# Projecting the first unit, and half of the last, with the weights stationary

## Chip, cores and metric

The kernel runs on one core of a Trainium2 chip. The metric is the device time of one execution in microseconds (us). Engines are named as in the profile: PE is TensorE, the matrix engine (PEld its weight loads), ACT is ScalarE, DVE is VectorE, POOL is GpSimd and SP is SyncE, which here issues transfers only.

## The reference

A causal convolution over 7 tokens, one softmaxed set of weights for each of 8 heads (24 channels each), and then a gated feed-forward layer. Input x is 8 x 4096 x 192 in float32, the output 32768 x 192.

```
w = softmax(weight)                               # 8 heads x 7 taps
x_pad = 6 rows of zeros ahead of each sequence of x
c[b,s,h,g] = sum_k w[h,k] * x_pad[b, s+k, h*24+g]
c = c.reshape(32768, 192)
out = (maximum(c @ w_gate, 0) * (c @ w_val)) @ w_out     # 192 -> 1536 -> 192
```

## The kernel before

Tokens go in 16 units (u = 0 to 15). A unit is 1024 tokens of one sequence and the same 1024 tokens of the sequence four batches on; the two are the "streams" st = 0, 1, kept in the upper and lower 64 partitions. A unit has two windows w of 512 tokens. The 1536 inner columns are NFF = 12 blocks f of 128.

*Gates* (gate_val, line 550). For each window and each f, six matmuls a stream (three 64-row chunks c for Wg, three for Wv) fill two tiles of PSUM. ACT takes the relu (line 561, tile gr), DVE multiplies it by the second tile (line 562) into hT, the inner activations, transposed. In units 1 to 14 the matmuls are cut into 64x64 tiles of the array (M = 64), in units 0 and 15 into 64x128 tiles (M = 128).

*Projection.* In units 1 to 14 (project_across) Wo is the stationary operand and hT moves, 512 tokens at a time, in 64x64 tiles: piece 0 gives the first 128 output columns of window 0, piece 1 those of window 1, piece 2 the last 64 columns of both. A piece has two turns (cross_pass, line 658): in each, the two halves of the rows write to different banks, and the second turn swaps the banks. Between the turns stands an empty instruction on SP that waits for the first turn's last matmul and lets the second start. The result comes out transposed, so it is copied as 16-bit words (line 680, "words"), written to a DRAM tile "held" (keep), read back by a transposing transfer (turn_back, line 698) and stored (send, line 708). Piece 1 is first copied raw by ACT and DVE (lines 736 and 737) and sorted into words by POOL during the next unit's gates. The transposing transfers and the stores are issued in the next unit, by SP in program order.

In units 0 and 15 (project) hT is stationary and Wo, 192 columns wide, moves (half_pass, line 579, 64x128 tiles); the result has tokens on partitions, is copied (evict, put, line 605) and stored (line 606) at once. The second window of unit 15 is done in whole 128x128 tiles (whole_half, line 628) at the very end, behind its first window's passes.

*Convolution.* For the next unit's tokens, ACT starts a sum (lane_first, line 508) and DVE continues it for the first 576 tokens of each unit (lane_rest, line 522); for the other 448, products of tap and shifted x are made by ACT, DVE (VECTOR, line 494) and, in unit 1, POOL (FOR_POOL), and POOL adds them (add, line 498) into xc. The shifted x comes from x_e, sorted by POOL into x_p (line 472) and transposed by SP's transfers into x_r (line 476). The last 448 tokens of unit 1 are instead convolved on PE during unit 0's projection, in two tiles "x" and "y" of two turns each (conv_turn_of, line 411), cast by ACT (conv_out, line 436) and transposed into xc by SP (conv_turn, line 460). The products' tile "prods" has one buffer, "x_h" (words and raws) two, PSUM four tiles "ps" of two banks.

The order on every engine is the order in which the code is written out; nothing is rescheduled. In unit 0 the projection runs: first window's stream 0 and the turns of the convolution mixed, then the other three, with ACT's products cut into portions (work).

Of the kernel before, what the change touches and what calls it, by code (L numbers as in the profile page):

```python
# [17 lines left out]
def kernel(  # L18
# [23 lines left out]
    WIN = 512  # L42
# [1 line left out]
    SUB = 112  # L44
    VECTOR = [(0, 5), (1, 5), (2, 5), (0, 6), (2, 1)]
    NOW = 2
    FOR_POOL = [(1, 6), (2, 6)]
    GSUB = 5
    DSUB = 104

# [349 lines left out]
    def conv_turn_of(g, t, wide, turn, after):  # L400


        xt = xts[g]
        n = len(GROUPS[g][1])
        W = 2 * n * G
        for slot in range(2):
            for r in range(2):
                bank = r ^ turn
                h = HEADS[t][bank][slot]
                rows = slice(64 * r, min(64 * r + 64, SUB + PAD))  # L410
                mm = nc.tensor.matmul(  # L411
                    out=wide[:, bank, W * slot : W * (slot + 1)],
                    lhsT=wide_bands[h][rows, :],
                    rhs=xt[rows, 0:n, :, G * h : G * (h + 1)],
                    start=(turn == 0 and slot == 0),
                    stop=(turn == 1),
                    tile_position=(64 * r, 0),
                    skip_group_check=True,
                )
                if after is not None:  # L420
                    tc.add_manual_dep(mm.ins, after.ins.name, SYNC, reason="same banks, other rows")
                    after = None
        if turn == 0:
            done = nc.sync.nop()
            tc.add_manual_dep(done.ins, mm.ins.name, SYNC, reason="first turn over")
            return done
# [105 lines left out]
            for c, k in VECTOR[:now]:  # L532
                product(nc.vector, v, c, k)

    def gate_val(u, w):
        h = hpool.tile([128, NFF, 2, WIN], F16, name="hT")
        xcb = xc[u]
        for f in range(NFF):
            if u == 0 and w == 0 and f == 5:
                second_block()  # L540
            pss = [psum.tile([128, 2, 512], FP, name="ps") for _ in range(2)]
            order = [(i, c) for i in range(2) for c in range(NCH)]
            if u == 0 and w == 0 and f == 0:
                order = [(i, c) for c in range(NCH) for i in range(2)]
            M = 64 if 0 < u < NUNIT - 1 else 128
            for i, c in order:
                W = (Wg, Wv)[i]
                for st in range(2):
                    for m in range(0, 128, M):
                        nc.tensor.matmul(  # L550
                            out=pss[i][m : m + M, st, :],
                            lhsT=W[64 * st : 64 * st + 64, c, 128 * f + m : 128 * f + m + M],
                            rhs=xcb[64 * st : 64 * st + 64, c, WIN * w : WIN * (w + 1)],
                            start=(c == 0),
                            stop=(c == NCH - 1),
                            tile_position=(64 * st, m),
                        )
            by_stream = u == 0 and w == 0 and f < 2
            for sts in (slice(0, 1), slice(1, 2)) if by_stream else (slice(0, 2),):
                gr = gpool.tile([128, 2, WIN], F16, name="gr")  # L560
                nc.scalar.activation(out=gr[:, sts], in_=pss[0][:, sts], func=ACTF.Relu)  # L561
                nc.vector.tensor_tensor(  # L562
                    out=h[:, f, sts], in0=gr[:, sts], in1=pss[1][:, sts], op=ALU.mult
                )
        return h
# [81 lines left out]
    def cross_pass(piece, hs, ps, turn, after):  # L647


        for f in range(NFF):  # L650
            for r in range(2):
                bank = r ^ turn
                for half in range(2):
                    if piece == 2:
                        w, st, d = bank, half, 128
                    else:
                        w, st, d = piece, bank, 64 * half
                    mm = nc.tensor.matmul(  # L658
                        out=ps[bank][64 * half : 64 * half + 64],
                        lhsT=Wo[64 * r : 64 * r + 64, f, d : d + 64],  # L660
                        rhs=hs[w][64 * r : 64 * r + 64, f, st, :],
                        start=(turn == 0 and f == 0),
                        stop=(turn == 1 and f == NFF - 1),
                        tile_position=(64 * r, 64 * half),
                        skip_group_check=True,
                    )
                    if after is not None:
                        tc.add_manual_dep(mm.ins, after.ins.name, SYNC, reason="same banks, other rows")
                        after = None
        return turn_over(turn, mm)  # L670
# [6 lines left out]
        return done  # L677

    def words(copy, pt, src):
        copy(out=pt[:], in_=src[:].bitcast(U16).rearrange("p b (t l) -> p b l t", l=2))  # L680

    def keep(u, i, pt):
        flat = pt[:].rearrange("p b l t -> p b (l t)")
        if i < 2:
            nc.sync.dma_start(
                out=planes[u][i, :, 0:128, :].rearrange("s c e -> c s e"), in_=flat
            )
            return
        for st in range(2):
            nc.sync.dma_start(  # L690
                out=planes[u][:, st, 128:D, :].rearrange("w c e -> c w e"),
                in_=flat[64 * st : 64 * st + 64],
            )

    def turn_back(u, i):
        w, st = i // 2, i % 2
# [7 lines left out]
    def send(u, i):  # L704
        w, st = i // 2, i % 2
        bp, w0 = u * UNIT // S, u * UNIT % S // WIN
        row0 = (bp + NB * st) * S + WIN * (w0 + w)
        nc.sync.dma_start(
            out=bass.AP(
                tensor=out.tensor,  # L710
                offset=out.offset + row0 * D,
                ap=[[D, 128], [128 * D, 4], [1, D]],
            ),
            in_=across.pop((u, i))[:],
        )

    def project_across(u, hs, work):
        planes[u] = dram.tile([2, 2, D, 2 * WIN], U16, name="held")
# [25 lines left out]
            for c, k in VECTOR[NOW:]:  # L744
                product(nc.vector, u + 1, c, k)

    def project(u, hs, work, y=None):
        bp, w0 = u * UNIT // S, u * UNIT % S // WIN
        at, done = {}, {}
        order = [(0, 0), (1, 0), (0, 1), (2, 0), (1, 1), (3, 0), (2, 1), (3, 1)]  # L750
        if u == 0:
            order = [(0, 0), ("x", 0), (1, 0), ("x", 1), ("y", 0), (0, 1), ("y", 1), (1, 1)]
            order += [(2, 0), ("out", 1), (3, 0), (2, 1), (3, 1)]
        if u == NUNIT - 1:
            order = [(0, 0), (1, 0), (0, 1), (1, 1), (2, 2), (3, 2)]
        rows0 = [(bp + NB * (i % 2)) * S + WIN * (w0 + i // 2) for i in range(4)]

        def fetch(i):
# [1 line left out]
                product(nc.scalar, u + 1, c, k)  # L760

        for i, turn in order:
            if i == "out":
                fetch(turn)
                evict(at[turn][0], rows0[turn], False)
                continue
            if i in ("x", "y"):
                t = int(i == "y")
                if turn == 0:
                    at[i] = psum.tile([128, 2, 512], FP, name="ps")  # L770
                elif t == 0:
                    fetch(0)
                done[i] = conv_turn_of(2, t, at[i], turn, done.get(i))
                if turn:
                    conv_out(2, t, at[i], y)
                continue
            h, st = hs[i // 2], i % 2
            row0 = rows0[i]
            if turn == 2:
# [1 line left out]
                continue  # L781
            if turn == 0:
                at[i] = slots()
            elif u > 0 or i > 1:
                fetch(i)
            done[i] = half_pass(h, st, at[i][1], turn, done.get(i))
            if turn and (u, i) != (0, 1):
                evict(at[i][0], row0, i == 3)


# [25 lines left out]
    for u in range(NUNIT):  # L816
# [8 lines left out]
        if 0 < u < NUNIT - 1:  # L825
            load_rest(lane_turn(u + 1))
        if u - 1 in planes:
            pt = ypool.tile([128, 2, 2, WIN], U16, name="y")
            words(nc.gpsimd.tensor_copy, pt, raws.pop(u - 1))
            keep(u - 1, 1, pt)  # L830
            turn_back(u - 1, 0)
            turn_back(u - 1, 1)
            send(u - 1, 0)
# [12 lines left out]
            for k in range(2, KW):  # L846
                add(u, k)
        while len(hs) < 2:
            hs.append(gate_val(u, len(hs)))
        del xc[u]  # L850
        work = [[] for _ in range(4)]
        if u + 1 < NUNIT:
            begun = lane_first(u + 1)
            if u == 0:
                flat = ypool.tile([128, ROOM], F16, name="y")
                y = flat[:, 0 : GSUB * NCH * 128].rearrange("p (j c s r) -> p j c s r", j=GSUB, c=NCH, s=2)
                load_rest(lane_load(2, begun))
            lane_rest(u + 1, len(VECTOR) if u in (0, NUNIT - 2) else NOW)
        if u + 2 < NUNIT:
            todo = [(c, k) for k in (0, 1, 2, 3, 4, 6) for c in range(NCH)]  # L860
            todo = [ck for ck in todo if ck not in VECTOR + (FOR_POOL if u == 0 else [])]
            cuts = [0, 5, 10, 15, 16] if u == 0 else [0, 10, 16, 16]
            work = [todo[a:b] for a, b in zip(cuts, cuts[1:])]
        if 0 < u < NUNIT - 1:
            project_across(u, hs, work)
        else:
            project(u, hs, work, y if u == 0 else None)
        if u == 0:
            conv_turn(2, y)

# [29 lines left out]
```

## Time and profile before

| | us |
|---|---|
| runs before | 762.23, 763.25, 769.23; median 763.25 |
| the profiled execution | 761.7 |
| its span on the core | 759.9 |
| PE busy | 756.1 (99%) |
| DVE busy | 707.4 (93%) |
| ACT busy | 617.3 (81%) |
| POOL busy | 404.9 (53%) |
| granted TensorE clock | 1.0 |

Busy times are those of the profiled execution. A PE that is busy all the time says that PE's work and its waits set the time; the other engines matter where PE waits for them. "A <- B" in a row names what ended an engine's idle time; the number behind x is a count of instructions.

### The profile page before, as it was taken

To read this page: it belongs to the slowest core of one execution; us is meant where nothing else is said; L and a number is where in the kernel's file an instruction comes from. 1 tells how busy PE (TensorE), PEld (TensorE's weight loads), DVE (VectorE), ACT (ScalarE), POOL (GpSimd) and SP (SyncE) were. 2 spreads that over 40 slices of the span, in tenths; PEclk is the share of its full clock that TensorE was granted. 3 is DMA by queue.
4 is the path that set the end of the run, shared out by engine and by line. 5 is a ranking of instruction groups with operands and counts; after the bars stand their busy time and mean duration, and the time that the engine had idled before them with its cause. 6 is when DMAs were issued, how large, how long until landed. Compare 5 with 4: busy or idle time off the path is not lost.

```text
span 759.9 us, 30608 instructions
## 1 busy us (share of the span) xinstructions
PE 756.1 (99%) x13623; PEld 484.0 (64%) x13623; DVE 707.4 (93%) x768; ACT 617.3 (81%) x719; POOL 404.9 (53%) x263
## 2 busy tenths in 40 slices
PE   9999999999999999999999999999999999999998
PEld 5495555555666666666666666666666776666548
DVE  7998999999999999999999999999999999999891
ACT  6887887978879798897988879788798887976671
POOL 9519449094580936819276291863908548091000
PEclk9999999999999999999999999999999999999999
DMA  9969029688395894949759498594957939654732
GB/s 118 132 113 136 16 68 157 162 107 181 94 184 146 91 180 105 190 128 105 195 93 184 119 138 180 81 186 114 170 145 100 189 98 160 140 107 113 185 87 85
DMA packets 231308, 100.33 MB, mean 132 GB/s; under 512 B 185288, under 2 KB 220424, under 8 KB 231176
## 3 DMA queue, kind: packets, MB, share of 16 engines
q1 hardware_dynamic: 189928, 82.71, 53.1%
q0 software_dynamic: 41104, 15.57, 20.7%
q8 instruction: 106, 1.74, 1.0%
q14 instruction: 26, 0.21, 0.1%
q10 hardware_dynamic: 144, 0.10, 0.0%
HBM read 31.48 MB, written 47.19 MB: 104 GB/s over the span
## 4 chain that ended last, share of the span: by engine, by line
PE 99%; ACT 0%; issue 0%
PE ps L550 66%; PE ps L658 29%; PE ps L579 3%; PE ps L628 1%; PE ps L154 0%; PE ps L370 0%; PE ps L309 0%; PE ps L411 0%; ACT acc L605 0%; PE ps L289 0%
## 5 line engine op out<-in xcount | busy, mean ns | idle before, releaser
L562 DVE TENSOR_TENSOR hT<-gr,ps 128x1024 f16<-128x1024 f16 (+1 forms) x386 | 469.0, 1216 | 30.0 <-ACT gr L561 3.3
L561 ACT ACTIVATE gr<-ps 128x1024 f16<-128x1024 f32 (+1 forms) x386 | 393.3, 1020 | 100.7 <-PE ps L550 100.3
L498 POOL TENSOR_TENSOR prods<-prods 128x1344 f32<-128x1344 f32 x70 | 212.9, 3042 | 268.7 <-DVE prods L494 265.3
L550 PE MATMUL ps<-xc,Wg 64*64 64x512 f16 (+1 forms) x4320 | 321.9, 376 | 0.0
L550 PE MATMUL ps<-xc,Wv 64*64 64x512 f16 (+1 forms) x4320 | 321.6, 376 | 0.0
L658 PE MATMUL ps<-hT,Wo 64*64 64x512 f16 x4032 | 220.3, 376 | 0.0
L550 PEld LDWEIGHTS <-Wg 64*64 64x64 f16 (+1 forms) x4320 | 154.0, 106 | 94.9 <-issue 0.7
L550 PEld LDWEIGHTS <-Wv 64*64 64x64 f16 (+1 forms) x4320 | 152.7, 105 | 95.8 <-issue 0.3
L658 PEld LDWEIGHTS <-Wo 64*64 64x64 f16 x4032 | 140.2, 107 | 77.4
L522 DVE SCALAR_TENSOR_TENSOR acc<-x_r,tap,acc 128x576 f32<-128x576 f16 x225 | 165.3, 814 | 0.0
L492 ACT ACTIVATE prods<-x_r,tap 128x448 f32<-128x448 f16 x222 | 127.2, 659 | 0.0
L680 ACT COPY x_h<-ps 128x2048 uint16<-128x2048 uint16 x28 | 51.8, 1848 | 8.8 <-PE ps L658 8.8
L208 POOL DMA_DIRECT2D x_e<-in_x_dram x58 | 46.9, 818 | 12.3 <-ACT acc L508 12.0
L472 POOL COPY x_p<-x_e 128x960 f16<-128x960 f16 (+1 forms) x58 | 50.5, 912 | 0.5 <-DMA x_e<-in_x_dram 0.5
L498 POOL TENSOR_TENSOR xc<-prods 128x1344 f16<-128x1344 f32 x14 | 42.5, 3037 | 1.1
L680 POOL COPY y<-x_h 128x2048 uint16<-128x2048 uint16 x14 | 26.6, 1897 | 23.3 <-ACT x_h L736 23.3
L522 DVE SCALAR_TENSOR_TENSOR xc<-x_r,tap,acc 128x576 f16<-128x576 f16 x45 | 34.1, 813 | 0.0
L508 ACT ACTIVATE acc<-x_r,tap 128x576 f32<-128x576 f16 x45 | 31.4, 765 | 0.0
L494 DVE TENSOR_SCALAR prods<-x_r,tap 128x448 f32<-128x448 f16 x70 | 27.7, 448 | 0.0
L579 PE MATMUL ps<-Wo,hT 64*128 64x192 f16 x576 | 24.6, 243 | 0.0
L579 PEld LDWEIGHTS <-hT 64*128 64x128 f16 x576 | 23.9, 94 | 0.5
L736 ACT COPY x_h<-ps 128x512 f32<-128x512 f32 x14 | 8.2, 587 | 10.9 <-ACT x_h L680 5.5
(62 smaller groups left out, 91.6 us busy)
## 6 DMA issues: line engine op xcount, KB each, us to landing
out_dram<-out_s SPq DMA_DIRECT2D x62, 384.0 KB
held<-x_h SPq DMA_DIRECT2D x14, 512.0 KB
held<-x_h SPq DMA_DIRECT2D x28, 256.0 KB
held<-y SPq DMA_DIRECT2D x14, 512.0 KB
x_e<-in_x_dram POOLq DMA_DIRECT2D x34, 192.0 KB, 6.7
x_e<-in_x_dram POOLq DMA_DIRECT2D x24, 240.0 KB, 5.4
x_r<-x_p SPq DMA_TRANSPOSE x131
out_s<-held SPq DMA_TRANSPOSE x56
```

The lines of the kernel that those rows point to most:

```text
L208: first = nc.gpsimd.dma_start(out=xe[:, j0 + start : j0 + n, st, :, :].rearrange("p j c r -> p j (c r)"), in_=bass.AP(tensor=x.tensor, off ...
L472: nc.gpsimd.tensor_copy(out=xp[:, j0 : j0 + n, :, st, :], in_=xe[:, j0 : j0 + n, st, :, :])
L492: engine.activation(out=out, in_=in_, func=ACTF.Copy, scale=scale)
L498: nc.gpsimd.tensor_tensor(out=pr[:, 0] if k < KW - 1 else xc[v + 1][:, :, LDVE:UNIT], in0=pr[:, 0], in1=pr[:, k], op=ALU.add,)
L508: nc.scalar.activation(out=accs[v][:, c, :], in_=shifted(v, c, 0, 0), func=ACTF.Copy, scale=tap[:, c, 0:1],)
L522: nc.vector.scalar_tensor_tensor(out=xc[v][:, c, 0:LDVE] if k == KW - 1 else acc[:, c, :], in0=shifted(v, c, k, 0), scalar=tap[:, c, k : k ...
L550: nc.tensor.matmul(out=pss[i][m : m + M, st, :], lhsT=W[64 * st : 64 * st + 64, c, 128 * f + m : 128 * f + m + M], rhs=xcb[64 * st : 64 * ...
L561: nc.scalar.activation(out=gr[:, sts], in_=pss[0][:, sts], func=ACTF.Relu)
L562: nc.vector.tensor_tensor(out=h[:, f, sts], in0=gr[:, sts], in1=pss[1][:, sts], op=ALU.mult)
L579: mm = nc.tensor.matmul(out=outs[q], lhsT=h[64 * r : 64 * r + 64, f, st, 128 * q : 128 * (q + 1)], rhs=Wo[64 * r : 64 * r + 64, f, :], sta ...
L658: mm = nc.tensor.matmul(out=ps[bank][64 * half : 64 * half + 64], lhsT=Wo[64 * r : 64 * r + 64, f, d : d + 64], rhs=hs[w][64 * r : 64 * r ...
L680: copy(out=pt[:], in_=src[:].bitcast(U16).rearrange("p b (t l) -> p b l t", l=2))
```

## The change

Unit 0 gets a routine of its own, project_first, in which Wo is stationary as in the middle units: pieces 0, 1 and 2 in 64x64 tiles, with the convolution's turns among them (also cut into 64x64 tiles); piece 2 writes into the banks of "x" and "y" that have been cast. Its results go through "held", with the raw copy sorted by POOL in unit 1, into a buffer "x_h". DVE makes two of its five products before the raw copy and three after it, as in the middle units; ACT has twelve products in place of fourteen, POOL four in place of two. Three empty PSUM allocations set which buffers the next gates get.

In the last unit the gates use M = 64, and the first window is projected by project_half: piece 0, and a piece 3 that takes the last 64 columns of both streams in halves of 256 tokens. It stands behind the first two gate groups of the second window instead of after all gates. The second window is projected at the end in whole tiles as before.

```diff
-    FOR_POOL = [(1, 6), (2, 6)]
+    FOR_POOL = [(0, 4), (1, 4), (1, 6), (2, 6)]
...
+                for m in (0, 64):                      # conv_turn_of
+                    mm = nc.tensor.matmul(
+                        out=wide[m : m + 64, bank, W * slot : W * (slot + 1)],
+                        lhsT=wide_bands[h][rows, m : m + 64],
...
-    def gate_val(u, w):
+    def gate_val(u, w, between=None):
...
+            if between is not None and f == 2:
+                between()
...
-            M = 64 if 0 < u < NUNIT - 1 else 128
+            M = 64 if u else 128
...
+                    if piece == 3:                     # cross_pass
+                        w, st, d = 0, bank, 128
+                        cols = slice(WIN // 2 * half, WIN // 2 * (half + 1))
...
+    def project_first(hs, work, y):
+        planes[0] = dram.tile([2, 2, D, 2 * WIN], U16, name="held")
+        tiles, done = {}, {}
+        order = [(0, 0), ("x", 0), ("y", 0), (1, 0), ("x", 1), ("y", 1), (0, 1), (2, 0), (1, 1), (2, 1)]
+        for i, turn in order:
...
+            if i == 2:
+                at = [tiles["x"][:, 0, :], tiles["y"][:, 1, :]]
+            else:
+                at = [tiles[i][:, n, :] for n in range(2)]
+            done[i] = cross_pass(i, hs, at, turn, done.get(i))
+            if turn == 0:
+                continue
+            for c, k in work[1 + i]:
+                product(nc.scalar, 1, c, k)
+            if i == 2:
+                raw = xpool.tile([128, 2, WIN], FP, name="x_h")
+                nc.scalar.copy(out=raw[:, 0, :], in_=at[0])
+                nc.vector.tensor_copy(out=raw[:, 1, :], in_=at[1])
+                raws[0] = raw
+            else:
+                pt = xpool.tile([128, 2, 2, WIN], U16, name="x_h")
+                words(nc.scalar.copy, pt, tiles[i])
+                keep(0, i, pt)
+        for c, k in VECTOR[NOW:]:
+            product(nc.vector, 1, c, k)
+        for _ in range(3):
+            psum.tile([128, 2, 512], FP, name="ps")
...
+    def project_half(u, hs):
...
+        for i, turn in [(0, 0), (3, 0), (0, 1), (3, 1)]:
...
+            done[i] = cross_pass(i, hs, at, turn, done.get(i))
+            if turn:
+                pt = xpool.tile([128, 2, 2, WIN // (1 if i == 0 else 2)], U16, name="x_h")
+                words(nc.scalar.copy, pt, tiles[i])
+                keep(u, i, pt)
+        for i in range(2):
+            turn_back(u, i)
+        for i in range(2):
+            send(u, i)
...
-            order = [(0, 0), (1, 0), (0, 1), (1, 1), (2, 2), (3, 2)]
+            order = [(2, 2), (3, 2)]
...
+            last = u == NUNIT - 1 and len(hs) == 1
+            hs.append(gate_val(u, len(hs), (lambda: project_half(u, hs)) if last else None))
...
-            lane_rest(u + 1, len(VECTOR) if u in (0, NUNIT - 2) else NOW)
+            lane_rest(u + 1, len(VECTOR) if u == NUNIT - 2 else NOW)
...
-            cuts = [0, 5, 10, 15, 16] if u == 0 else [0, 10, 16, 16]
+            cuts = [0, 5, 6, 12, 12] if u == 0 else [0, 10, 16, 16]
```

In the changed file the gates' matmuls stand at line 553, the cross passes' at 665, the relu at 564, hT at 565, POOL's adds at 499, word copies at 688 and whole_half at 631.

More of the change, by code (lines that the diff above doesn't have):

```diff
@@ L410, in conv_turn_of @@
                 rows = slice(64 * r, min(64 * r + 64, SUB + PAD))
[L411 to L422, printed above, removed]
+                for m in (0, 64):
+                    mm = nc.tensor.matmul(
+                        out=wide[m : m + 64, bank, W * slot : W * (slot + 1)],
+                        lhsT=wide_bands[h][rows, m : m + 64],
+                        rhs=xt[rows, 0:n, :, G * h : G * (h + 1)],
+                        start=(turn == 0 and slot == 0),
+                        stop=(turn == 1),
+                        tile_position=(64 * r, m),
+                        skip_group_check=True,
+                    )
+                    if after is not None:
+                        tc.add_manual_dep(mm.ins, after.ins.name, SYNC, reason="same banks, other rows")
+                        after = None
         if turn == 0:
@@ L653, in cross_pass @@
                 for half in range(2):
-                    if piece == 2:
+                    cols = slice(0, WIN)
+                    if piece == 3:
+                        w, st, d = 0, bank, 128
+                        cols = slice(WIN // 2 * half, WIN // 2 * (half + 1))
+                    elif piece == 2:
                         w, st, d = bank, half, 128
@@ L658, in cross_pass @@
                     mm = nc.tensor.matmul(
-                        out=ps[bank][64 * half : 64 * half + 64],
+                        out=ps[bank][64 * half : 64 * half + 64, 0 : cols.stop - cols.start],
                         lhsT=Wo[64 * r : 64 * r + 64, f, d : d + 64],
-                        rhs=hs[w][64 * r : 64 * r + 64, f, st, :],
+                        rhs=hs[w][64 * r : 64 * r + 64, f, st, cols],
                         start=(turn == 0 and f == 0),
@@ L679, in words @@
     def words(copy, pt, src):
-        copy(out=pt[:], in_=src[:].bitcast(U16).rearrange("p b (t l) -> p b l t", l=2))
+        n = pt.shape[-1]
+        copy(out=pt[:], in_=src[:, :, 0:n].bitcast(U16).rearrange("p b (t l) -> p b l t", l=2))
     def keep(u, i, pt):
@@ L688, in keep @@
             return
[L689 to L693, printed above, removed]
+        for n in range(2):
+            if i == 2:
+                nc.sync.dma_start(
+                    out=planes[u][:, n, 128:D, :].rearrange("w c e -> c w e"),
+                    in_=flat[64 * n : 64 * n + 64],
+                )
+                continue
+            for st in range(2):
+                dst = planes[u][0, st, 128:D, :].rearrange("c (l t) -> c l t", l=2)
+                nc.sync.dma_start(
+                    out=dst[:, :, WIN // 2 * n : WIN // 2 * (n + 1)],
+                    in_=pt[64 * n : 64 * n + 64, st],
+                )
     def turn_back(u, i):
@@ L715, in send @@
         )
+    def project_first(hs, work, y):
[3 more added lines that the diff above has]
+        for i, turn in order:
+            if turn == 0 and i != 2:
+                tiles[i] = psum.tile([128, 2, 512], FP, name="ps")
+            if i in ("x", "y"):
+                t = int(i == "y")
+                if turn and not t:
+                    for c, k in work[0]:
+                        product(nc.scalar, 1, c, k)
+                done[i] = conv_turn_of(2, t, tiles[i], turn, done.get(i))
+                if turn:
+                    conv_out(2, t, tiles[i], y)
+                continue
+            if i == 2:
[4 more added lines that the diff above has]
+            if turn == 0:
+                continue
+            for c, k in work[1 + i]:
+                product(nc.scalar, 1, c, k)
+            if i == 2:
+                raw = xpool.tile([128, 2, WIN], FP, name="x_h")
[10 more added lines that the diff above has]
+            psum.tile([128, 2, 512], FP, name="ps")
     def project_across(u, hs, work):
@@ L745, in project_across, with project @@
                 product(nc.vector, u + 1, c, k)
-    def project(u, hs, work, y=None):
+    def project_half(u, hs):
+        planes[u] = dram.tile([2, 2, D, 2 * WIN], U16, name="held")
+        tiles, done = {}, {}
+        for i, turn in [(0, 0), (3, 0), (0, 1), (3, 1)]:
+            if turn == 0:
+                tiles[i] = psum.tile([128, 2, 512], FP, name="ps")
+            at = [tiles[i][:, n, :] for n in range(2)]
+            done[i] = cross_pass(i, hs, at, turn, done.get(i))
+            if turn:
+                pt = xpool.tile([128, 2, 2, WIN // (1 if i == 0 else 2)], U16, name="x_h")
[5 more added lines that the diff above has]
+            send(u, i)
+    def project(u, hs, work):
         bp, w0 = u * UNIT // S, u * UNIT % S // WIN
@@ L750, in project @@
         order = [(0, 0), (1, 0), (0, 1), (2, 0), (1, 1), (3, 0), (2, 1), (3, 1)]
-        if u == 0:
-            order = [(0, 0), ("x", 0), (1, 0), ("x", 1), ("y", 0), (0, 1), ("y", 1), (1, 1)]
-            order += [(2, 0), ("out", 1), (3, 0), (2, 1), (3, 1)]
         if u == NUNIT - 1:
-            order = [(0, 0), (1, 0), (0, 1), (1, 1), (2, 2), (3, 2)]
+            order = [(2, 2), (3, 2)]
         rows0 = [(bp + NB * (i % 2)) * S + WIN * (w0 + i // 2) for i in range(4)]
@@ L762, in project @@
         for i, turn in order:
[L763 to L776, printed above, removed]
             h, st = hs[i // 2], i % 2
@@ L783, in project @@
                 at[i] = slots()
-            elif u > 0 or i > 1:
+            else:
                 fetch(i)
             done[i] = half_pass(h, st, at[i][1], turn, done.get(i))
-            if turn and (u, i) != (0, 1):
+            if turn:
                 evict(at[i][0], row0, i == 3)
@@ L827 @@
         if u - 1 in planes:
-            pt = ypool.tile([128, 2, 2, WIN], U16, name="y")
+            pool, name = (xpool, "x_h") if u == 1 else (ypool, "y")
+            pt = pool.tile([128, 2, 2, WIN], U16, name=name)
             words(nc.gpsimd.tensor_copy, pt, raws.pop(u - 1))
-            keep(u - 1, 1, pt)
+            keep(u - 1, 2 if u == 1 else 1, pt)
             turn_back(u - 1, 0)
@@ L848 @@
         while len(hs) < 2:
-            hs.append(gate_val(u, len(hs)))
+            last = u == NUNIT - 1 and len(hs) == 1
+            hs.append(gate_val(u, len(hs), (lambda: project_half(u, hs)) if last else None))
         del xc[u]
@@ L861 @@
             todo = [ck for ck in todo if ck not in VECTOR + (FOR_POOL if u == 0 else [])]
-            cuts = [0, 5, 10, 15, 16] if u == 0 else [0, 10, 16, 16]
+            cuts = [0, 5, 6, 12, 12] if u == 0 else [0, 10, 16, 16]
             work = [todo[a:b] for a, b in zip(cuts, cuts[1:])]
-        if 0 < u < NUNIT - 1:
+        if u == 0:
+            project_first(hs, work, y)
+        elif u < NUNIT - 1:
             project_across(u, hs, work)
         else:
-            project(u, hs, work, y if u == 0 else None)
+            project(u, hs, work)
         if u == 0:
```

## The prediction

> **What bounds the kernel now.** I read the shares of the engines and the chain that ended last first, then the chain piece by piece at its two ends, where the change lies, then timelines of the places at which work is handed over.
>
> ```profile
> PE 756.1 (99%) x13623; PEld 484.0 (64%) x13623; DVE 707.4 (93%) x768; ACT 617.3 (81%) x719; POOL 404.9 (53%) x263
> PE 99%; ACT 0%; issue 0%
> ```
>
> TensorE (PE) is busy for 756.1 of 759.9 us and the chain that sets the end is PE alone. So only two things move the time: PE's own work, and any moment in which PE must wait. The chain in order of time gives PE's price of each stage (start, us, what):
>
> ```profile
> 0.78 2.72 PE ps L154 x6
> ...
> 3.68 0.54 PE ps L154
> ...
> 5.28 1.95 PE ps L370 x117
> ...
> 40.31 1.98 PE ps L579 x48
> 42.28 0.17 PE ps L411 x4
> 42.45 1.98 PE ps L579 x48
> 44.43 0.33 PE ps L411 x8
> 44.77 1.98 PE ps L579 x48
> 46.75 0.17 PE ps L411 x4
> 46.91 9.90 PE ps L579 x240
> 56.82 31.20 PE ps L550 x576
> 88.02 15.54 PE ps L658 x288
> 103.56 31.09 PE ps L550 x576
> ...
> 709.74 31.19 PE ps L550 x288
> 740.92 7.92 PE ps L579 x192
> 748.84 8.04 PE ps L628 x96
> ```
>
> A middle unit costs 31.09 (gates) + 15.54 (projection, Wo stationary: 288 matmuls, so 2.59 us for a turn of 48). Unit 0 projects with hT stationary from 40.31 to 56.82, 16.51 us, of which 0.17 + 0.33 + 0.17 = 0.67 are the convolution's turns. The last unit pays 31.19 for gates, 7.92 for its first window, 8.04 for its second. Both ways of projecting already run close to the array's rate, so there is little to win.
>
> **Part 1, unit 0's projection.** All matmuls become the 64x64 form, 288 of them at the middle units' price, 15.54; the turns' 16 matmuls become 32 half as wide and, four at a time instead of two, should take the same 0.67. Sum 16.21 for 16.51: -0.30 us.
>
> That holds if nobody makes PE wait; these rows say when ScalarE (ACT) and VectorE (DVE) get to the new copies:
>
> ```profile
> 40.62 2.10 ACT L508 ACTIVATE acc<-x_r,tap 128x576 f32<-128x576 f16 x3
> 45.41 0.83 ACT L436 CAST y<-ps 112x384 f16<-112x384 f32 x2
> 47.48 0.93 ACT L436 CAST y<-ps 112x384 f16<-112x384 f32 x3
> 52.84 2.27 DVE L522 SCALAR_TENSOR_TENSOR xc<-x_r,tap,acc 128x576 f16<-128x576 f16 x3
> 58.42 5.86 SPq L460 DMA_TRANSPOSE xc<-y  x4
> 90.34 5.70 ACT L492 ACTIVATE prods<-x_r,tap 128x448 f32<-128x448 f16 x10
> 101.05 1.85 ACT L680 COPY x_h<-ps 128x2048 uint16<-128x2048 uint16 x1
> 103.68 0.59 ACT L736 COPY x_h<-ps 128x512 f32<-128x512 f32 x1 [0.78 <-PE ps L658]
> ```
>
> ACT's new order: lane start to 42.7, five products at 0.57 to 45.5, the turns' five casts (0.83 + 0.93, after the second turns' end at 46.15) to about 47.9, one product, the first word copy when its pass ends at 48.75, to 50.6, six products to 54.1, the second word copy to 56.0, the raw copy when PE ends at 56.52, to 57.2. PE asks for that last bank with its second gate group at 57.8: 0.6 us in hand. Piece 2 reuses the turns' banks at 48.75, 0.9 us after the casts. DVE ends its lane at 55.1 as before, makes two products, the raw copy when PE ends, and the three products that it now defers. Word copies, raw copies and deferral stand as in the middle units, whose chain shows no gap. So cost 0. Without this cover each late us would be a us of PE.
>
> **Part 2, narrow moving operands.** The trace has no 64x64 matmul narrower than 512. The turns are 192 wide, piece 3 (the last unit's third of 128 columns) 256: four matmuls stream in 81 or 107 ns, and four weight loads must fit beside them. Nearest row from above: line 579, 41.2 ns for a load of 128 columns (1.98 us / 48); were 64 columns no cheaper, four take 165 ns, costing 24 x 58 ns + 8 x 84 ns = 2.06 us. From below: line 370 pairs load and matmul in 16.7 ns (1.95 / 117, up to 32 columns), so four fit. I take 0: scaled by columns, 41.2 becomes 20.6 and four need 82. The range keeps 2.06.
>
> By the Trainium skill, page "TensorE: Matmul & The Clock Gate", section "LDWEIGHTS (loading the stationary operand)", a load takes its columns divided by 1.2 ns, 53 ns here, which speaks against the change: with two loads in series per row half, 107 ns per four, that would add 0.2 us to the turns (an estimate). The row of line 370 does not agree: 32 columns would be 27 ns by it, and the pairs come every 16.7.
>
> **Part 3, POOL in unit 1.** Two more products go to POOL in unit 1, and so does the word copy of unit 0's raw tile, as in the middle units. Unit 3 of before shows a middle unit's chain on POOL, from its first add to its last:
>
> ```profile
> 152.22 3.04 POOL L498 TENSOR_TENSOR prods<-prods 128x1344 f32<-128x1344 f32 x1 [18.30 <-DVE prods L494]
> 176.19 3.04 POOL L498 TENSOR_TENSOR xc<-prods 128x1344 f16<-128x1344 f32 x1
> L494 POOL TENSOR_SCALAR prods<-x_r,tap 128x448 f32<-128x448 f16 x2 | 2.8, 1434 | 0.0
> ```
>
> Unit 3 began at 103.56 + 31.09 + 15.54 = 150.19 on PE, so the chain runs from +2.03 to +29.04. Four products at 1.434 make it end at +34.8 in unit 1. ACT writes the next products into the same buffer from 90.34, which is +33.5 in unit 1, and it must wait for that last add: 1.3 us late. Behind the waiting instruction stand ten products, the word copy, six more, the next word copy (to 102.90 before) and the raw copy, which itself waited 0.78 for PE; so the raw copy is 0.5 late, ending at 104.75, and the word copy ends at 104.2. Unit 2's gates want these banks at 104.21 (0.65 into the group from 103.56) and 104.86. Price: 0 to 0.2, I take 0.1; from there every further us that POOL is late is a us. Bounds: 0 if POOL's copy overlaps its DMA waits; 1.8 if a second word copy's worth (1.9 us) is lost.
>
> **Part 4, SP.** Unit 0's 4 stores become 4 writes to "held", 4 transposes out of it and 4 stores, moved into unit 1 behind the 4 transposes of y and 9 of x_r. Those of y now go once the second word copy is done (56.0), not at 58.42, and with 5.86 us land well ahead of the second window's gates (56.5 + 15.5). The signals that let a second turn start are queued on SP:
>
> ```profile
> SPq L675 <- PE ps L658: 81.5, 42, 13.2
> 134.13 0.51 SPq L708 DMA_DIRECT2D out_dram<-out_s  x1
> 720.88 3.16 SPq L698 DMA_TRANSPOSE out_s<-held  x1
> 724.37 3.40 SPq L708 DMA_DIRECT2D out_dram<-out_s  x2
> ```
>
> So far SP waits for PE (42 times), not PE for SP. In unit 2 SP is through with the stores at 134.13, +30.6; unit 1 will need its first signal by +36.3 (31.09 + two turns), leaving 5.7 us, as much as y's four transposes take (5.86) if they came wholly on top; they end at 62.3, ahead of x_r's. Cost 0.
>
> **Part 5, the last unit.** Gates in 64x64 tiles: 31.09 for 31.19, -0.10. The first window's projection: 96 x 512 wide (5.18) and 96 x 256 wide (2.59), 7.77 for 7.92: -0.15. But it moves from the end to behind the second gate group of the second window, and that opens two waits. The rows of the old end:
>
> ```profile
> 734.90 7.70 DVE L562 TENSOR_TENSOR hT<-gr,ps 128x1024 f16<-128x1024 f16 x6
> 740.32 1.02 ACT L561 ACTIVATE gr<-ps 128x1024 f16<-128x1024 f32 x1 [0.27 <-PE ps L550]
> 748.77 7.87 PEld L628 LDWEIGHTS <-hT 128*128 128x128 f16 x96 [0.16 <-issue]
> ```
>
> *Tail.* Gates end at 740.93; the last hT slice is done at 742.60, 1.67 later. The old first-window passes (7.92 us) covered this. Now the second window's projection, 84 ns a matmul, follows directly: its twelfth matmul wants the last slice 0.92 after the gates, so PE waits 0.75, and the waiting weight load (7.87 / 96 = 0.08) comes on top: +0.85 with the handing over.
>
> *Behind the inserted passes.* ACT gets the word copies 6.5 us into the 7.77 (1.85, to 8.4, then half as much, to 9.3), so the relu of the next group starts at 9.3 instead of 8.5, its hT (1.26, from 741.34 to 742.60 above) ends at 11.6, and the bank it frees is wanted at 11.0: +0.65, once. With two gate groups (2.59) and the first slices ahead of it, the inserted pass itself finds the last slice of window 0 ready. Its stores, ready near 737, need a chain of held, transpose and send, with some 20 us left.
>
> Sum: -0.30 - 0.10 - 0.15 + 0.1 + 0.85 + 0.65 = +1.05, say +1.0 us. Span 759.9 to 760.9; the profiled execution's 761.7 (1.8 around the span) to 762.7. It is below the three runs shown (762.23, 763.25, 769.23); the median of all four is 762.7, and by it the forecast is 763.7.
>
> **Rivals.**
> 1. *The new waits stay hidden*: the tail or the relu is shorter, only the -0.55 remains, 762.2, or part of it. For it: ACT idles 0.27 a group. Against: the order of instructions leaves nothing between the last gate and the second window. 0.10.
> 2. *Narrow passes bound by weight loads*: +2.06, 765.8. For: line 579's load of 41.2 ns. Against: line 370's 16.7. 0.09.
> 3. *POOL later than reckoned*: another 1.8 us, 765.5. For: it waits for "x_h" to be stored. Against: the middle units' copy waits for nothing. 0.09.
> 4. *Slower, over 1%: SP late in the last unit.* The second turn there starts 3.9 us into the inserted passes, about 731.5, behind a signal queued after unit 14's stores, issued until 727.8. If SP is over 3.8 us late, each us is a us of PE. At 8 us late PE idles 4.2, and the first rows of the chain show PE after idleness: 0.45 to 0.54 us for a 512 wide matmul that later takes 0.22. The rest of the passes (3.9 us) at half pace adds as much: 8.1 and the sum's 1.0, 771.8; from about 6.5 us late it is over 1%. For: one transpose takes 3.16 us. Against: it needs all four so slow. 0.07 with a run like 769.23.
>
> By the Trainium skill, page "TensorE: Matmul & The Clock Gate", section "What's actually happening", PE falls to half clock after an idle window of some 3.4 us; the waits of 0.85 and 0.65 reckoned here stay under it, and no row before the end shows such a fall.
>
> The forecast keeps 0.63. Faster by over 1% (7.6 us, about what a measurement of this kernel can tell from no change) has no mechanism, since PE loses 0.55 us of work at most: 0.02 for the spread of runs. Slower by over 1%: 0.07. Within 1%: 0.91. The range, 761.2 to 767.6, reaches from rival 1 less the distance of the lowest execution to the median (1.0) up to rivals 2 and 3 together (763.7 + 2.06 + 1.8).
>
> **What would show it.** Right: the chain has L665 at 15.54 with the turns between from about 40.3 to 56.5; 7.77 among the last gates; a PE wait near 0.65 about three groups later and one near 0.85 in the twelfth matmul of line 631; ACT's first product in unit 1 waiting for POOL by 1.3. Wrong: turns over 0.67 or piece 3 over 2.59 (part 2), a gap at 56 to 60 (part 1), a gap at 104 to 106 over 0.3 (part 3), PE waiting for SP (part 4), no gap at the tail (part 5).

## The result and the profile after

The changed kernel took 764.69 us in the median of 14 runs, the kernel before 762.19 in 14: a ratio of 1.0036 (95% interval 1.0020 to 1.0051), 2.5 us slower. Its profiled execution took 764.7 us with a span of 762.9, 3.0 more than the span of before. Forecast were 763.7, +1.0: the sign held, the size was two and a half times as large.

The chain of the changed kernel that ended last, in order of time (start, us, what), around the two ends of the change:

```profile
40.56 2.71 PE ps L665 x48
43.28 0.33 PE ps L412 x16
43.61 2.59 PE ps L665 x48
46.20 0.33 PE ps L412 x16
46.53 10.36 PE ps L665 x192
56.89 31.08 PE ps L553 x576
87.97 15.58 PE ps L665 x288
103.56 0.91 DVE xc L523 x2
...
106.88 1.14 DVE hT L565
...
108.07 28.04 PE ps L553 x516
136.10 15.54 PE ps L665 x288
...
711.31 18.13 PE ps L553 x336
729.44 6.51 PE ps L665 x144
...
740.99 9.28 PE ps L553 x168
...
752.63 7.20 PE ps L631 x85
```

Stage by stage, before and after, from the starts in the two chains:

| stretch | before | after | difference | forecast |
|---|---|---|---|---|
| up to unit 0's projection | 40.31 | 40.56 | +0.25 | 0 |
| unit 0's projection and unit 1's gates | 47.71 | 47.41 | -0.30 | -0.30 |
| unit 1's projection and unit 2's gates | 46.63 | 48.13 | **+1.50** | +0.1 |
| from there to the last unit | 575.09 | 575.21 | +0.12 | 0 |
| last unit to PE's end | 47.14 | 48.52 | +1.38 | +1.25 |

The chain of before was PE alone; here it leaves PE at 103.56 for DVE's convolution of unit 2, and PE goes on without a break only from 108.07. One row of the lane sums (DVE's part of the convolution, lane_rest: smallest, median and largest duration in ns, then the first and last start) tells why, the changed kernel's in this fence, that of before in the next:

```profile
L523 DVE SCALAR_TENSOR_TENSOR acc<-x_r,tap,acc x15: 801/802/2507, 89.6 to 101.5; 128x576 f32<-128x576 f16 x15
```

```profile
L522 DVE SCALAR_TENSOR_TENSOR acc<-x_r,tap,acc x15: 811/815/817, 89.6 to 99.8; 128x576 f32<-128x576 f16 x15
```

One of fifteen sums took 2507 ns instead of 802. The timeline of the changed kernel shows it to be the first, and what ran beside it (below it, POOL's last add of unit 1 in the kernel before):

```profile
88.41 3.05 POOL L499 TENSOR_TENSOR xc<-prods 128x1344 f16<-128x1344 f32 x1
89.57 4.69 DVE L523 SCALAR_TENSOR_TENSOR acc<-x_r,tap,acc 128x576 f32<-128x576 f16 x4
91.49 5.71 ACT L493 ACTIVATE prods<-x_r,tap 128x448 f32<-128x448 f16 x10 [1.10 <-POOL xc L499]
104.52 0.41 PE L553 MATMUL ps<-xc,Wg 64*64 64x512 f16 x4 [0.32 <-DVE xc L523]
105.85 0.84 PE L553 MATMUL ps<-xc,Wg 64*64 64x512 f16 x12 [0.27 <-DVE x_h L792]
```

```profile
82.33 3.04 POOL L498 TENSOR_TENSOR xc<-prods 128x1344 f16<-128x1344 f32 x1
```

POOL's last add of unit 1 ends at 91.46, as late as forecast (+34.6 in the unit, for +34.8), and ACT waits 1.10 us for it, as forecast (1.3). But DVE's sum, begun at 89.57, also ends only at 92.08, 0.6 us behind that add. In the kernel before the add was over at 85.37, 4.2 us ahead of the sum. DVE is then 1.7 us late, and it is DVE's xc, raw copy and next hT, not ACT's copies, for which PE waits.

### The profile page after: what moved, and what is told of

It reads as the page before. It is cut to its first block, busy times and chain, and to the rows that moved or that the text cites. A ratio compares the mean times of both kernels' runs of the same rounds, so it can differ in the third digit from the quotient of the medians.

```text
span 762.9 us, 31040 instructions
## 1 busy us (share of the span) xinstructions
PE 756.9 (99%) x13831; PEld 492.6 (65%) x13831; DVE 709.0 (93%) x768; ACT 618.9 (81%) x716; POOL 409.4 (54%) x266
## 4 chain that ended last, share of the span: by engine, by line
PE 97%; DVE 1%; ACT 1%; DMA 0%; issue 0%; POOL 0%; POOLq 0%; ACTq 0%
PE ps L553 64%; PE ps L665 31%; PE ps L631 1%; DMA x_h<-in_x_dram 0%; DVE hT L565 0%; PE ps L370 0%; ACT gr L564 0%; DVE prods L495 0%; ACT x_h L688 0%; DVE xc L523 0%; POOL x_h L134 0%; PE ps L412 0%; DVE x_h L792 0%; ACT acc L608 0%; POOL steps L133 0%
## 5 line engine op out<-in xcount | busy, mean ns | idle before, releaser
L553 PE MATMUL ps<-xc,Wg 64*64 64x512 f16 (+1 forms) x4464 | 325.7, 376 | 0.7 <-DVE xc L523 0.3
L553 PE MATMUL ps<-xc,Wv 64*64 64x512 f16 (+1 forms) x4464 | 325.1, 376 | 0.5 <-DVE hT L565 0.4
L665 PE MATMUL ps<-hT,Wo 64*64 64x512 f16 (+1 forms) x4512 | 244.4, 374 | 0.0
L553 PEld LDWEIGHTS <-Wg 64*64 64x64 f16 (+1 forms) x4464 | 164.5, 107 | 86.0 <-issue 1.8
L553 PEld LDWEIGHTS <-Wv 64*64 64x64 f16 (+1 forms) x4464 | 156.9, 106 | 93.1 <-issue 1.9
L665 PEld LDWEIGHTS <-Wo 64*64 64x64 f16 x4512 | 158.9, 107 | 81.9 <-issue 0.4
L523 DVE SCALAR_TENSOR_TENSOR acc<-x_r,tap,acc 128x576 f32<-128x576 f16 x225 | 167.0, 821 | 0.0
L688 ACT COPY x_h<-ps 128x2048 uint16<-128x2048 uint16 (+1 forms) x32 | 58.3, 1825 | 15.4 <-PE ps L665 15.4
L792 DVE COPY x_h<-ps 128x512 f32<-128x512 f32 x14 | 9.7, 691 | 1.9 <-ACT x_h L688 0.8
L631 PE MATMUL ps<-Wo,hT 128*128 128x192 f16 x96 | 8.3, 246 | 0.7 <-DVE hT L565 0.7
```

Source lines behind the costliest of these rows:

```text
L523: nc.vector.scalar_tensor_tensor(out=xc[v][:, c, 0:LDVE] if k == KW - 1 else acc[:, c, :], in0=shifted(v, c, k, 0), scalar=tap[:, c, k : k ...
L553: nc.tensor.matmul(out=pss[i][m : m + M, st, :], lhsT=W[64 * st : 64 * st + 64, c, 128 * f + m : 128 * f + m + M], rhs=xcb[64 * st : 64 * ...
L665: mm = nc.tensor.matmul(out=ps[bank][64 * half : 64 * half + 64, 0 : cols.stop - cols.start], lhsT=Wo[64 * r : 64 * r + 64, f, d : d + 64] ...
L688: copy(out=pt[:], in_=src[:, :, 0:n].bitcast(U16).rearrange("p b (t l) -> p b l t", l=2))
```

## The experiments

Three readings stood against each other for the 1.50. **L**: POOL's add holds up DVE's sum. **A**: ACT's wait for POOL is what costs, as the prediction had it. **C**: the transfers of unit 0's results, new in unit 1, slow DVE. The other runs take the two waits of the last unit. Where no ratio is given, a run was executed once and is read by its profile alone.

**pool2** gives POOL its two products back and ACT the other two.

```diff
-    FOR_POOL = [(0, 4), (1, 4), (1, 6), (2, 6)]
+    FOR_POOL = [(1, 6), (2, 6)]
-            cuts = [0, 5, 6, 12, 12] ...
+            cuts = [0, 5, 8, 14, 14] ...
```

> The changed kernel, but POOL keeps its two products in unit 1, and ACT makes the other two in unit 0 (three instead of one before the first word copy). POOL's last add of unit 1 then ends 2 x 1.43 = 2.9 us earlier, about 88.6, before DVE's first lane sum at 89.6. Theory L (POOL's add, reading SBUF, holds up DVE's lane sum, which took 2.5 instead of 0.8 us): all lane sums at 0.8, and the stretch from unit 1's projection to the end of unit 2's gates shrinks from 48.13 to 46.6 us. Theory A (ACT's wait of 1.1 us for POOL is what costs): the same 46.6, since that wait goes too. Rival C (the transfers of unit 0's results, new in unit 1, slow DVE): 48.1 as before. Unit 0's projection stays at 16.3 if ACT's two products fit, up to 16.9 if not. Span 761.3 by L or A, 762.9 by C.

Lane sums and chain of that run:

```profile
L523 DVE SCALAR_TENSOR_TENSOR acc<-x_r,tap,acc x15: 808/809/811, 91.4 to 101.6; 128x576 f32<-128x576 f16 x15
```

```profile
50.55 7.96 PE ps L665 x142
58.51 31.28 PE ps L553 x576
89.79 15.54 PE ps L665 x288
105.33 31.08 PE ps L553 x576
136.41 15.54 PE ps L665 x288
```

The stretch is back at 46.62 and no sum is long: C falls, since the transfers are all there. The span did not fall, though (763.0): unit 1 began at 58.51, not 56.89. In this execution ACT waited 2.7 us for the transposed x of unit 1, the casts behind ACT's five products came late, and PE, which needs the casts' banks for piece 2, waited. I take that for chance, since the edit changes nothing ahead of that transfer, and last_only, whose unit 0 is that of before, met it too: ACT waited 2.9 us there, and PE lost 0.6 us to it, 1.1 here (from the starts in the two timelines).

**act_free** keeps four products on POOL and lets ACT make those of taps 1 to 4 first.

```diff
-            todo = [(c, k) for k in (0, 1, 2, 3, 4, 6) for c in range(NCH)]
+            ks = (1, 2, 3, 4, 0, 6) if u == 1 else (0, 1, 2, 3, 4, 6)
+            todo = [(c, k) for k in ks for c in range(NCH)]
```

> The changed kernel with four products on POOL, but in unit 1 ACT makes the products of taps 1 to 4 first and those of taps 0 and 6 after them, so that its first product no longer writes what POOL's last add still reads. ACT's wait of 1.1 us goes, the overlap of POOL's last add with DVE's first lane sum stays. Theory L: first lane sum still 2.5 us, the stretch from unit 1's projection to the end of unit 2's gates stays at 48.1 (47.9 to 48.2), span 762.9. Theory A: 46.6 to 46.8, span 761.4.

Inconclusive: the stretch took 48.12 (87.84 to 135.96), but ACT's wait of 1.1 us stayed. The products lie in one buffer, which seems to change hands as a whole; so it was built again with two.

**act_free2** has the order of act_free and a buffer of its own for taps 0 and 6.

```diff
-    room = apool.tile([128, KW, NCH, LPOOL], FP, name="prods")
+    room = apool.tile([128, 5, NCH, LPOOL], FP, name="prods")
...
+            prods[v] = apool.tile([128, 5, NCH, LPOOL], FP, name="prods"), apool.tile([128, 2, NCH, LPOOL], FP, name="firsts")
...
```

> As act_free, whose ACT still waited 1.1 us for POOL's last add, because the products of all taps lie in one buffer that is handed over as a whole. Here the products of taps 1 to 5 have a buffer of their own, and in unit 1 ACT makes those of taps 1 to 4 first, so ACT's wait for POOL should be gone from the list of waits (below 0.1 us), with POOL's last add of unit 1 still running until about 91.4, into DVE's first lane sum. Theory L: that sum takes 2.5 us, the stretch from unit 1's projection to the end of unit 2's gates 47.9 to 48.2 us, as in the changed kernel. Theory A: 46.6 to 46.8.

Timeline and chain of that run:

```profile
88.17 3.05 POOL L499 TENSOR_TENSOR xc<-firsts 128x1344 f16<-128x1344 f32 x1
89.36 12.69 DVE L523 SCALAR_TENSOR_TENSOR acc<-x_r,tap,acc 128x576 f32<-128x576 f16 x15
90.09 5.69 ACT L493 ACTIVATE prods<-x_r,tap 128x448 f32<-128x448 f16 x10
```

```profile
87.77 15.58 PE ps L665 x288
103.35 0.89 DVE xc L523 x2
...
107.84 28.04 PE ps L553 x516
135.88 4.28 PE ps L665 x77
```

ACT starts its products at 90.09 without waiting, DVE's fifteen sums still take 12.69 us (the longest 2476 ns), and the stretch stays at 48.11. A falls: the wait that I had priced costs nothing, the one that I had not seen costs all 1.5.

**before_pool6** puts the same lateness into the kernel before.

```diff
-    FOR_POOL = [(1, 6), (2, 6)]
+    FOR_POOL = [(0, 4), (1, 4), (2, 4), (2, 3), (1, 6), (2, 6)]
-            cuts = [0, 5, 10, 15, 16] ...
+            cuts = [0, 5, 10, 10, 10] ...
```

> The kernel before, with six products on POOL in unit 1 instead of two and four fewer on ACT in unit 0. Nothing else of the change is in it. POOL's last add of unit 1 then ends at 85.4 + 4 x 1.42 = 91.1 instead of 85.4, past DVE's first lane sum at 89.6. Theory L: that sum takes about 2.1 instead of 0.8 us and unit 1's projection with unit 2's gates take about 47.8 instead of 46.6. Theory A: ACT waits 0.7 for POOL, which its slack before the raw copy (0.8) takes up, and the stretch stays at 46.6 to 46.7. Rival C: 46.6, since the transfers are those of before.

```profile
L522 DVE SCALAR_TENSOR_TENSOR acc<-x_r,tap,acc x15: 802/804/1866, 89.8 to 101.1; 128x576 f32<-128x576 f16 x15
```

The first sum takes 1866 ns, 1.06 more than the median, and the stretch 47.50 us (88.21 to 135.71), 0.87 more, with ACT waiting only 0.5. Nothing else of the change is in this kernel. L holds, a little below its 47.8, as the overlap was shorter than reckoned.

**last_only** is the kernel before with the changed last unit (project_half, M = 64, and the order of the second window alone at the end).

> The kernel before with the last unit of the changed kernel, unit 0 as it was. If the two ends of the change add up, from the start of the last unit's gates to the end of PE 48.5 us as in the changed kernel, against 47.1 before: +1.4, with a wait of about 0.7 behind the inserted passes and one of about 0.9 at the twelfth matmul of the second window's projection. Span 761.3. If instead the last unit's waits came from the lateness handed down from unit 2, 47.0 and span 759.7.

From 710.40 to 758.92, 48.52 us: exactly the changed kernel's. The two ends add up, and nothing is handed down from unit 2. (The span was 762.0 and not 761.3, again from a late x in unit 0.)

**dve_words** takes ACT's second copy behind the inserted passes away.

```diff
-                words(nc.scalar.copy, pt, tiles[i])
+                words(nc.vector.tensor_copy if i == 3 else nc.scalar.copy, pt, tiles[i])
```

> The changed kernel, but in the last unit DVE instead of ACT copies the words of piece 3 out of PSUM. Reason given in the prediction for the wait behind the inserted passes: ACT has two word copies (2.8 us) ahead of the next relu, so the relu comes 0.7 late. Expected by it: the relu of the next group starts about 738.0 minus what earlier stages gain, 0.7 sooner, the first gate matmul that waited for hT does not wait, and from the start of the inserted passes to the last gate 20.7 to 20.8 us instead of 21.4; span 762.3. Rival: the wait comes from PE's change of work itself or DVE's copy is as late (DVE then delays hT instead): 21.3 to 21.5.

Timeline of the run, then of the changed kernel at the same place:

```profile
737.29 1.23 DVE L688 COPY x_h<-ps 128x1024 uint16<-128x1024 uint16 x1 [6.24 <-PE ps L665]
750.06 1.08 PE L631 MATMUL ps<-Wo,hT 128*128 128x192 f16 x11
```

```profile
735.98 2.78 ACT L688 COPY x_h<-ps 128x2048 uint16<-128x2048 uint16 x2 [6.11 <-PE ps L665]
738.64 3.00 ACT L564 ACTIVATE gr<-ps 128x1024 f16<-128x1024 f32 x3
740.99 0.84 PE L553 MATMUL ps<-xc,Wv 64*64 64x512 f16 x12 [0.41 <-DVE hT L565]
750.83 1.08 PE L631 MATMUL ps<-Wo,hT 128*128 128x192 f16 x11
```

The inserted passes start at 729.38 here and at 729.44 there, so from their start to the last gate it is 20.68 us against 21.39. The 0.71 is the relu that stood behind ACT's copies, as reckoned.

**tail** lets the first tile of each half use the last slice last.

```diff
+            turns = [(b, f) for b in range(n) for f in range(NFF)]
+            if n == 2:
+                turns = [(b, f) for b, f in turns if f < NFF - 1] + [(b, NFF - 1) for b in range(n)]
+            for b, f in turns:
...
```

> The changed kernel, but in the first tile of each half of the second window's projection both token blocks run through the slices 0 to 10 and only then through the last one, so that the last slice is wanted 22 matmuls (1.85 us) after the gates instead of 11 (0.92). Reason given in the prediction for the tail's wait: the last slice is done 1.7 us after the gates. Expected by it: the wait of 0.9 goes to 0 or 0.1, these 96 matmuls take 8.1 us from the last gate instead of 9.0, span 762.0. Rival: the wait is one for the array's change from 64x64 to 128x128 tiles or for a bank: it stays at 0.7 to 0.9, elsewhere.

The projection of the second window in this run, and in the changed kernel (each in its own timeline):

```profile
750.52 8.09 PE L633 MATMUL ps<-Wo,hT 128*128 128x192 f16 x96
```

```profile
752.63 7.19 PE L631 MATMUL ps<-Wo,hT 128*128 128x192 f16 x85 [0.72 <-DVE hT L565]
```

There PE runs eleven matmuls from 750.83 and then waits; here all 96 run through. From start to end 8.1 us against 9.0: the wait was for the last hT slice, not for a bank or the change of tile form.

**pool2b** is pool2 with ACT's two products placed one before the casts and one before the raw copy (cuts of 0, 6, 7, 13, 14), timed in 12 runs.

> The changed kernel with two products on POOL in unit 1 and ACT's two products placed one before the casts of the convolution and one before the raw copy. Theory L: first lane sum of unit 1 at 0.8 us, units 1 and 2 back to 46.6, so 1.5 us less than the changed kernel and 1.2 us more than the kernel before: ratio to before 1.0015 (1.000 to 1.003). If POOL's part is not what costs, ratio 1.0036 as the changed kernel.

763.45 us against 762.48 for the kernel before: ratio 1.0012 (1.0002 to 1.0023). The longest sum is 814 ns and the stretch 46.63. The interval still touches that of the changed kernel (from 1.0020), so it is the profile that shows the gain.

**first_only** is pool2b with the last unit of before.

> Unit 0 of the changed kernel with two products on POOL in unit 1, and the last unit of the kernel before. By the terms of the sum that are left, unit 0's projection 16.2 to 16.3 for 16.5 us and nothing else: -0.3 us, ratio to before 0.9996 (0.999 to 1.001); unit 1's and 2's stages as before, 46.6 each. If unit 0's new form hands on another wait, the ratio is 1.001 to 1.003 and a gap stands in units 1 or 2.

```profile
40.84 2.71 PE ps L665 x48
...
46.81 10.36 PE ps L665 x192
57.17 31.08 PE ps L553 x576
88.25 15.54 PE ps L665 x288
103.80 31.09 PE ps L553 x576
```

No wait is left and the projection takes 16.33; its timing, 1.0007 (0.9980 to 1.0033), can't tell 0.3 us from none.

**best** and **best_again** are one kernel: pool2b, dve_words and tail together.

> The changed kernel with all three waits taken away: two products on POOL in unit 1 (ACT makes the other two in unit 0: one before the casts, one before the raw copy), DVE copying the words of piece 3, the last slice last in the second window. By theory L and the two reasons of the ends: 48.1 to 46.6 in units 1 and 2, -0.7 behind the inserted passes, -0.85 at the tail, in all -3.0 us against the changed kernel and -0.3 against the kernel before: ratio to before 0.9996 (0.998 to 1.001). If the gains are given back elsewhere (ACT in unit 0, a late x_r at the start), 1.001 to 1.003.

> The kernel with all three waits taken away once more, on another occasion, since one disturbed execution (770.4) widened its interval. Expected -0.3 us by the sum of the terms, -1.0 by the medians of the first time: ratio 0.9990 to 0.9997. The profile should show no wait of PE from unit 1 on and 16.2 to 16.3 us in unit 0's projection if the transposed x of unit 1 lands before 43 us.

761.51 against 762.48 (ratio 0.9996, 0.9976 to 1.0016) and 762.21 against 762.85 (0.9986, 0.9972 to 1.0000). From the last unit on, the chain of best_again has no wait:

```profile
719.61 18.13 PE ps L553 x336
737.74 7.80 PE ps L667 x192
745.54 12.95 PE ps L553 x240
758.49 8.04 PE ps L633 x96
```

It beats the changed kernel (their intervals against the kernel before don't meet). Its medians lie 0.6 to 1.0 us under the kernel before, but the intervals reach 1.0016 and 1.0000, so a gain over that is not shown.

## Why the prediction was right, and where it was not

- *The total*: five of the six terms of the sum came out within 0.1 us, and the sign held by part 5. The sixth was missed by 1.4. That the time lies in the range all the same is luck: the range was wide enough because of rivals 2 and 3, and neither of them happened.
- *Part 1, -0.30*: measured -0.30, but over two stages, -0.18 in the projection and -0.12 in unit 1's gates. The first turn takes 2.71 instead of 2.59, and unit 1's gates 31.08 instead of 31.20: 0.12 us goes with the change of tile form and moved with it, which the prediction counted in neither place. The order on ACT ran as written (second word copy at 54.35 to 56.2).
- *Part 2, 0*: the turns take 0.33 for 16, 20.6 ns each, and the inserted passes 7.80 for 7.77. The rival of weight-bound passes (+2.06) is out. By the Trainium skill, page "TensorE: Matmul & The Clock Gate", section "LDWEIGHTS (loading the stationary operand)", a load takes 53 ns here; the prediction's 107 for four of them, two in series, is not borne out, since four fit into 82 ns. Whether a load is shorter or more of them go side by side, no run here separates. Line 370 could not settle it: only 60 of its first 120 pairs load 32 columns, the others 8 to 24, and they go to four column positions of the array in turn.
- *Part 3, +0.1*: **the step that failed**; it measured +1.50, and the gap at 104 to 106, named as its sign of being wrong, came. Its timing of POOL and of ACT's wait was right, but it followed only who waits by a signal. That POOL's add could hold up DVE, beside PE the engine with the least to spare (93% busy), was put at nothing: rival 3 gave "POOL later than reckoned" its 1.8 us, while POOL was on time and DVE paid. By the Trainium skill, page "SBUF — State Buffer", section "Who interferes with whom", a DVE instruction with two inputs in SBUF contends with a GpSimd instruction that reads SBUF, and whichever issues second waits for the first to finish. The traces agree in every run: 2454 to 2507 ns in the five profiles with four products on POOL, 1866 in before_pool6, where POOL's add ran into the first of these sums, and at most 817 in the other seven, where it did not; each long sum ended 0.6 us behind the add. Read beside the timeline, this page would have given an overlap of 2.0 for part 3: POOL until +34.8, DVE's first sum from 89.6, which was +32.8 in unit 1.
- *Part 4, 0*: no PE wait names SP.
- *Part 5, +1.25 in the last unit*: it measured +1.38; the two waits measured 0.71 (for 0.65) and 0.9 (for 0.85), and dve_words and tail show their causes to be those named.
- The early +0.25 and the +0.12 in the middle belong to no step. Unit 0's projection began between 40.3 and 40.5 in the three profiles with unit 0 as before, between 40.4 and 41.9 in the ten with the change. I take the first for chance; that is not shown.

## What to carry to other kernels

When work is moved to an engine with time to spare, price what it then runs beside, not only who waits for its result: here 2.9 us of products on a half-idle POOL, whose other new work in unit 1 had left it 0.9 us ahead of DVE's sums (first_only), cost 1.5 us of PE, by way of DVE. A block that is pulled ahead of the end to hide its own output uncovers what it used to cover; look for the last dependency behind it, and put the part that needs it last. In this kernel, whose bound engine never waited, a better form of a few per cent of its work was worth tenths of a microsecond, and each new wait cost more than that.

## What the runs showed of the hardware beyond that

- Not everything on DVE is held up: its hT products, which read one operand from PSUM, ran beside POOL's adds at their usual pace (none of the 386 over 1223 ns), and its sums beside POOL's issuing of transfers (11.02 us for fifteen, as in other units). Two rows each from the changed kernel's timeline, DVE and POOL:

```profile
83.25 6.40 DVE L565 TENSOR_TENSOR hT<-gr,ps 128x1024 f16<-128x1024 f16 x5
82.17 6.16 POOL L499 TENSOR_TENSOR prods<-prods 128x1344 f32<-128x1344 f32 x2
42.15 11.02 DVE L523 SCALAR_TENSOR_TENSOR acc<-x_r,tap,acc 128x576 f32<-128x576 f16 x15
42.19 3.20 POOL L208 DMA_DIRECT2D x_e<-in_x_dram  x4 [10.92 <-ACT acc L509]
```

- When the first transposed x lands varies by some 8 us between profiled executions. ACT began its products on it at 43.28 in first_only and at 50.28 in best, whose unit 0 is the same, and at 51.42 in best_again (771.41 us): there ACT waited 8.0 us for it and PE 6.3 for the casts behind ACT. Why the transfer is late at times stays open. The wait had a second price: the granted clock, 1.00 before it, was 0.50 from 55.6 to 60.0 us and 0.61 to 62.0, and PE took 10.44 us for the part of the projection that took 7.96 in pool2. That is the loss of pace which rival 4 of the prediction reckoned with for another place. The wait (us in total, times, longest) and the piece of the chain behind it:

```profile
PE ps L667 <- ACT y L437: 6.3, 2, 6.1
56.48 10.44 PE ps L667 x134
```
